# Sliding-window attention into a SwiGLU block: the first output projection by chunks of the weights, for four row groups at once

## The chip, the cores and the metric

The kernel runs on one core of a Trainium2 chip. The metric is the device time of one execution in microseconds, lower is better. A core has five engines, each with its own instruction stream: TensorE (PE, matmul; its weight loads are shown as PEld), VectorE (DVE), ScalarE (ACT), GpSimd (POOL) and SyncE (SP). They meet only through semaphores. DMA transfers are issued from the streams of POOL, SP and ACT and run beside all of them. Matmuls write to PSUM, which here is cut into eight banks of 128 x 512 float32.

## The reference

```python
# q, k, v: (8 batches, 8 heads, 576 rows, 64); float32
scores = q @ k.T / sqrt(64)                 # per batch and head
mask   = (0 <= i - j) & (i - j < 64)        # causal window of 64
attn   = softmax(where(mask, scores, -1e9)) @ v
x      = attn.transpose(0, 2, 1, 3).reshape(4608, 512)
g      = x @ w_gate                          # 512 x 1536
out    = ((g * sigmoid(g)) * (x @ w_val)) @ w_out    # w_out: 1536 x 512
```

## The kernel before, in words

The 4608 rows are worked in nine tiles of 512 (`NT = 9`). Tile t is the first 512 rows of a batch; one tile (`LAST`, t = 7) collects the last 64 rows of all eight batches. The program says "batch t" for tile t. Every instruction stream runs in the order in which the program is written (`manual_schedule`); there is no planner. Data of a tile waits only where a semaphore says so, and a buffer or PSUM bank is taken up again only when its last reader is done.

**One tile.** The eight heads go in four pairs u. `scores` (L207) multiplies the turned queries and keys of a pair into PSUM, takes the exponential on ACT into `E` and multiplies by a 0/1 mask on DVE. `totals` (L249) multiplies `E` by ones and so gets the row sums, spread over the 64 columns of a head; `log` and `invert` (L258, L261) turn them to 1/sum on ACT as exp(-ln). `mix` (L271) multiplies `E` by v, `scale` (L282) applies 1/sum on DVE and writes a quarter of `xT`; `values` is both. v is held twice: `v1` as loaded, `v2` shifted by 64 rows, since a window reaches over two blocks of 64. `gate_value` (L325) computes one of 12 columns of 128 of both gate products from `xT` in four chunks c, into a `g_ps` and a `v_ps` bank; `gate_end` (L317) makes `hT` from them with Silu (ACT) and a product (DVE). `project` (L362) multiplies `hT` by `wo` for one of four row groups s, 12 chunks of 128 into one bank `o_ps`; `project_end` (L343) copies the bank to `os_` on DVE and stores it from SP.

**PSUM.** Pool `ps_f` has two banks tagged "g" and two tagged "v" (used by g_ps, v_ps, o_ps, and by d_ps, which holds the row sums); pool `ps_a` has two tiles of two banks each, tagged "a" (scores, ao_ps, and d_ps where `wide` or `one` asks for it). Tags rotate.

**Tile 0** is the opening. The scores, totals and values are written out by hand, with `keep_warm` matmuls, whose result nobody reads, where PE would wait. From L513: the log of pair 2's sums, the shifts of v for pairs 0 to 2, values 0 and 1, the shift for pair 3, five warm-ups, chunk 0 of the first gate column, the sums of pair 3, chunk 0 of the second gate column, values 2, chunk 1 of both, values 3, chunk 2, chunk 3. Then the rest of the 12 gate columns (L533 on). Among them DVE turns the queries of batch 1 with `turn_q` (L188), after gate columns 9, 10 and 11.

**Between tile 0 and tile 1** (L557 to L574) the first projection is threaded with the attention of batch 1: scores 0 and 1; chunks 0 to 5 for row groups 0 and 1; scores 2 and 3; chunks 6 to 11 for them; the sums of pairs 0 and 1 one by one; row group 2; the sums of pairs 2 and 3 with all four mixes and scales (`finish_values`, L297); row group 3. In every later tile the loop (L576 on) does the same with whole row groups.

**Queues.** The gate weights, the keys and queries of later batches, `wo` and the v of batches 1 and 2 are issued from POOL, whose order is: gate weights, keys of batch 1, queries of batch 1 (L87), `wo` in three thirds of four chunks (L492 to L494), v of batch 1 in four parts (L495), then queries, keys and v of batch 2. POOL's transfers use eight semaphores in turn, so that each issue waits for the landing of the one eight issues earlier. SP issues the first inputs, and later the stores of the results.

Of the kernel before, what the change touches and what calls it, by code (L numbers as in the profile page):

```python
# [8 lines left out]
P = 128  # L9
FP32 = mybir.dt.float32  # L10
# [7 lines left out]
def kernel(  # L18
# [10 lines left out]
    nc = tc.nc  # L29
# [12 lines left out]
    fsb = ctx.enter_context(tc.tile_pool(name="fsb", bufs=3))  # L42
    hpool = ctx.enter_context(tc.tile_pool(name="hpool", bufs=2))
    ps_a = ctx.enter_context(tc.tile_pool(name="ps_a", bufs=2, space=PSUM))
    ps_f = ctx.enter_context(tc.tile_pool(name="ps_f", bufs=2, space=PSUM))
# [5 lines left out]
    v1 = [cst.tile([P, 4, H, D], BF16, name=f"v1{i}") for i in range(2)]  # L51
# [9 lines left out]
    def batch(t):  # L61
        return t if t < LAST else t - 1
# [7 lines left out]
    staged, queries, weights, inverse, xT, hT = {}, {}, {}, {}, {}, {}  # L70
# [55 lines left out]
    def load_v(eng, dst, t, which=range(4)):  # L126
        for i in which:
            eng.dma_start(  # L128
                dst[:, i], v[batch(t), :, P * i:P * i + P].rearrange("h r d -> r h d")
            )  # L130
# [15 lines left out]
    def cast_v(t, which=range(4), copy=nc.gpsimd.tensor_copy):  # L146
        for i in which:
            copy(v1[t % 2][:, i], staged[t, "v"][:, i])  # L148

    def shift_pair(t, u):  # L150
        hs = slice(2 * u, 2 * u + 2)
        a, b = v1[t % 2][:, :, hs], v2[t % 2][:, :, hs]
        nc.vector.tensor_copy(b[64:128, 1:4], a[64:128, 0:3])
        nc.vector.tensor_copy(b[0:64], a[0:64])

    def shift_v(t, copy, lo=0, hi=4):

        a, b = v1[t % 2], v2[t % 2]
        top = min(hi, 3)
        if top > lo:  # L160
            copy(b[64:128, lo + 1:top + 1], a[64:128, lo:top])
        copy(b[0:64, lo:hi], a[0:64, lo:hi])
# [8 lines left out]
    def weights_o(c0, c1):  # L171
        nc.gpsimd.dma_start(
            wo[:, c0:c1, :],
            moe_w_out[P * c0:P * c1].rearrange("(c r) f -> r c f", r=P),
        )
# [73 lines left out]
    def totals(t, u, d_ps):  # L249
        for h in range(2):  # L250
            nc.tensor.matmul(  # L251
                d_ps[64 * h:64 * h + 64], ones[:, 0:D], weights[t, u][:, h, :]
            )

    def room(n):
        return fsb.tile([P, 2, 512], FP32, name="r", tag="r", bufs=4)[:, 0:n]

    def log(r, d_ps):  # L258
        nc.scalar.activation(r, d_ps, AF.Ln)  # L259

    def invert(r):  # L261
        nc.scalar.activation(r, r, AF.Exp, scale=-1.0)  # L262

    def sums(t, u, d_ps):
        totals(t, u, d_ps)
        r = room(1)[:, 0]
        log(r, d_ps)
        invert(r)
        inverse[t, u] = r

    def mix(t, u, o_ps):  # L271
        E = weights.pop((t, u))
        for m in range(8):
            for h in range(2):
                nc.tensor.matmul(  # L275
                    blocks(o_ps[64 * h:64 * h + 64], t, m, m + 1),
                    (v1, v2)[m // 4][t % 2][:, m % 4, 2 * u + h, :] if t == LAST
                    else (v2, v1)[m % 2][t % 2][:, m // 2, 2 * u + h, :],
                    blocks(E[:, h, :], t, m, m + 1),
                )  # L280

    def scale(t, u, o_ps):  # L282
        if u == 0:
            xT[t] = att.tile([P, 4, 512], BF16, name="xT", tag="xT")
        nc.vector.tensor_mul(xT[t][:, u, :], o_ps, inverse.pop((t, u)))  # L285

    def values(t, u, o_ps):
        mix(t, u, o_ps)
        scale(t, u, o_ps)

    def wide(name):
        return ps_a.tile([P, 2, 512], FP32, name=name, tag="a")

    def d_tile():
        return ps_f.tile([P, 512], FP32, name="d_ps", tag="v")[:]

    def finish_values(t):  # L297
        for u in (2, 3):
            sums(t, u, d_tile())
        tiles = wide("ao_ps"), wide("ao_ps")  # L300
        for u in range(4):
            mix(t, u, tiles[u // 2][:, u % 2])
        for u in range(4):
            scale(t, u, tiles[u // 2][:, u % 2])

    def gate_part(t, ms, tiles, c):
        for m, pair in zip(ms, tiles):
            for ps, w in zip(pair, (wg, wv)):
                nc.tensor.matmul(
                    ps[:], w[:, c, P * m:P * m + P], xT[t][:, c, :],  # L310
                    start=(c == 0), stop=(c == 3),
                )

    def gate_tiles():
        return [ps_f.tile([P, 512], FP32, name=x + "_ps", tag=x) for x in "gv"]
# [19 lines left out]
    def project_part(t, ss, tiles, cs):  # L335
        for c in cs:
            for s, o_ps in zip(ss, tiles):
                nc.tensor.matmul(  # L338
                    o_ps[:], hT[t][:, c, P * s:P * s + P], wo[:, c, :],
                    start=(c == 0), stop=(c == 11),  # L340
                )

    def project_end(t, s, o_ps):  # L343
        os_ = fsb.tile([P, 512], FP32, name="os_", tag="os_", bufs=3)
        nc.vector.tensor_copy(os_[:], o_ps[:])
        rows = out[S * batch(t):S * batch(t) + 512]
        if t < TURNED:
            nc.sync.dma_start(rows.rearrange("(r e) f -> e r f", e=4)[s], os_[:])
            return
        if t == LAST:  # L350
            rows = out.rearrange("(b s) f -> b s f", s=S)[:, 512:S]
            rows = rows.rearrange("b (r e) f -> e b r f", e=16)
        else:
            rows = rows.rearrange("(r e) f -> e r f", e=16)
        for i in range(4):
            eng = nc.scalar if t == NT - 1 and i % 2 else nc.sync
            eng.dma_start(rows[4 * s + i], os_[32 * i:32 * i + 32])

    def out_tile():
        return ps_f.tile([P, 512], FP32, name="o_ps", tag="g")  # L360

    def project(t, s):  # L362
        o_ps = out_tile()
        project_part(t, (s,), (o_ps,), range(12))
        project_end(t, s, o_ps)

    def project_last(t, s):
        rows = out[S * batch(t):S * batch(t) + 512].rearrange("(r e) f -> e r f", e=16)
        os_ = fsb.tile([P, 512], FP32, name="os_", tag="os_", bufs=3)
        tiles = out_tile(), out_tile()  # L370
        for x in range(2):
            f = slice(256 * x, 256 * x + 256)
            for c in range(12):
                nc.tensor.matmul(  # L374
                    tiles[x][:, 0:256], hT[t][:, c, P * s:P * s + P], wo[:, c, f],
                    start=(c == 0), stop=(c == 11),
                )
            nc.vector.tensor_copy(os_[:, f], tiles[x][:, 0:256])
            for i in range(4):
                eng = nc.scalar if i % 2 else nc.sync  # L380
                eng.dma_start(rows[4 * s + i][:, f], os_[32 * i:32 * i + 32, f])
# [4 lines left out]
    def set_silu():  # L386
        nc.scalar.preload_act_table_set("silu_and_others")
# [18 lines left out]
    def keep_warm(n):  # L406
        for _ in range(n):
            nc.tensor.matmul(warm[0:D], ones[:, 0:D], ones[:])
# [32 lines left out]
    on_v, on_p, on_a = nc.vector.tensor_copy, nc.gpsimd.tensor_copy, nc.scalar.copy  # L441
# [49 lines left out]
    load_qk(1)  # L491
    weights_o(0, 4)  # L492
    weights_o(4, 8)
    weights_o(8, 12)  # L494
    load_v(nc.gpsimd, v1[1], 1)  # L495
    cast_v(0, (0, 1), on_v)
    scores(0, 2)
    turn_pe(3)
    d_ps, r = wide("d_ps"), room(2)
# [7 lines left out]
    def log_of(u):  # L507
        d_ps = one("d_ps")
        totals(0, u, d_ps)
        inverse[0, u] = room(1)[:, 0]  # L510
        log(inverse[0, u], d_ps)
# [2 lines left out]
    log_of(2)  # L514
    for u in range(2):
        shift_pair(0, u)
    shift_pair(0, 2)
    for u in range(2):
        values(0, u, ps_f.tile([P, 512], FP32, name="ao_ps", tag="gv"[u])[:])
    shift_pair(0, 3)  # L520
    keep_warm(5)
    pairs = [gate_tiles() for _ in range(2)]
    gate_part(0, (0,), pairs, 0)
    log_of(3)
    for u in (2, 3):
        invert(inverse[0, u])
    gate_part(0, (1,), pairs[1:], 0)
    for u in (2, 3):
        values(0, u, one("ao_ps"))
        gate_part(0, (0, 1), pairs, u - 1)  # L530
    gate_part(0, (0, 1), pairs, 3)
    set_silu()
    for m in range(12):  # L533
        if m < 2:
# [10 lines left out]
        if 5 <= m < 9:  # L545
            u = m - 5
            join(on_a, keys[:, u], raw_k[:, 2 * u:2 * u + 2])
        if 6 <= m < 10:
            u = m - 6
# [5 lines left out]
    turn_q(1, 3)  # L555

    set_exp()  # L557
    halves = out_tile(), out_tile()
    for u in range(4):
        scores(1, u)  # L560
        if u % 2:
            project_part(0, (0, 1), halves, range(3 * u - 3, 3 * u + 3))
    for s in range(2):
        project_end(0, s, halves[s])
    load_qk(2)
    load_v(nc.gpsimd, v1[0], 2)
    for i in range(4):
        shift_v(1, on_v, i, i + 1)

    for u in range(2):  # L570
        sums(1, u, d_tile())
    project(0, 2)
    finish_values(1)
    project(0, 3)  # L574

    for t in range(1, NT):  # L576
        if t > 1:
# [71 lines left out]
```

## Time and profile before

| what | value |
|---|---|
| median of 5 runs | 334.01 us (333.92 to 334.25) |
| the profiled execution's own time | 334.25 us |
| its span, first to last instruction | 332.3 us |
| granted TensorE clock, mean | 0.997 |
| PE busy | 325.9 us of the span |
| opening: start of the third gate column (m = 2) | 20.75 us |
| end of the gate columns of tile 0, start of scores 0 of batch 1 | 39.00 us |
| start of the gate columns of batch 1 | 54.15 us |
| from one tile's projection to the next, later tiles | 34.7 us (75.6, 110.3, 145.0, 179.7) |

A line of a timeline gives the start (us from the span's start), the duration, the engine, the line in the kernel, the operation with out<-in, the number of instructions merged into it, and in brackets the idle time ahead of it and what ended that. A matmul's duration reaches past the start of the next one, since they are pipelined: for a row of n matmuls the start of the next row says more than the duration. A DMA line gives the issuing queue, the number of issues, KB each, and the time from issue to landing.

### The profile page before, as it was taken

The numbers are of one execution on the slowest core, as the hardware profiler recorded it, in microseconds if no ns is written. First come the engines' busy times: TensorE is split into PE (matmuls) and PEld (weight loads), VectorE is DVE, ScalarE is ACT, GpSimd is POOL, SyncE is SP. The second block draws the span as 40 slices with busy tenths as digits, with TensorE's granted clock in tenths as the row PEclk, the third lists the DMA queues.
The fourth block names the chain that finished last, engine by engine and source line by source line (L and its number), as shares of the span: only waits on it lengthen the run. The fifth ranks groups of instructions, "written<-read, shape, count | busy, mean of one in ns | idle before, by whom it ended". The sixth has DMA issues, their size and how long they took to land.

```text
span 332.3 us, 7009 instructions
## 1 busy us (share of the span) xinstructions
PE 325.9 (98%) x2747; PEld 154.7 (47%) x2747; DVE 212.5 (64%) x326; ACT 168.2 (51%) x241; POOL 140.5 (42%) x249
## 2 busy tenths in 40 slices
PE   8999999999999999999999999999999999999995
PEld 4444435444544454445444544444444544454443
DVE  5855765586566755875678566856785576754431
ACT  5765555338533853377336743565347533953310
POOL 4954444936848984556024995264200000000000
PEclk9999999999999999999999999999999999999998
DMA  7999999999999679859922999199401320020013
GB/s 257 195 193 201 207 187 241 111 190 220 183 225 193 80 133 250 150 75 218 190 62 30 166 206 143 15 189 190 99 0 40 89 56 2 21 77 32 2 34 95
DMA packets 83249, 43.59 MB, mean 131 GB/s; under 512 B 63888, under 2 KB 77968, under 8 KB 83216
## 3 DMA queue, kind: packets, MB, share of 16 engines
q0 software_dynamic: 50416, 23.08, 56.3%
q1 hardware_dynamic: 31776, 19.02, 21.1%
q10 hardware_dynamic: 1024, 1.05, 1.1%
q8 instruction: 21, 0.34, 0.4%
q14 instruction: 12, 0.10, 0.1%
HBM read 54.00 MB, written 9.44 MB: 191 GB/s over the span
## 4 chain that ended last, share of the span: by engine, by line
PE 86%; DMA 9%; POOL 3%; issue 0%; SPq 0%; DVE 0%; POOLq 0%
PE o_ps L338 28%; PE g_ps L329 25%; PE v_ps L329 25%; DMA k_r<-in_k_dram 4%; DMA wo<-in_moe_w_out_dram 4%; PE s_ps L233 3%; PE d_ps L251 3%; PE ao_ps L275 2%; DMA q_f<-in_q_dram 1%; POOL wv L166 1%; POOL wg L166 1%; PE o_ps L374 1%; POOL v L128 1%; POOL qk_b L447 0%; POOL k_r L73 0%
## 5 line engine op out<-in xcount | busy, mean ns | idle before, releaser
L322 ACT ACTIVATE sg<-g_ps 128x512 f32<-128x512 f32 x108 | 64.4, 597 | 117.5 <-PE g_ps L329 87.5
L323 DVE TENSOR_TENSOR hT<-sg,v_ps 128x512 bf16<-128x512 f32 x108 | 74.7, 692 | 60.9 <-PE v_ps L329 59.8
L329 PE MATMUL g_ps<-xT,wg 128*128 128x512 bf16 x424 | 108.8, 379 | 0.0
L329 PE MATMUL v_ps<-xT,wv 128*128 128x512 bf16 x424 | 108.8, 379 | 0.0
L338 PE MATMUL o_ps<-wo,hT 128*128 128x512 bf16 x420 | 95.5, 380 | 0.4 <-DMA wo<-in_moe_w_out_dram 0.4
L107 POOL DMA_DIRECT2D k_s<-in_k_dram x112 | 60.6, 555 | 34.4 <-DMA q_s<-in_q_dram 22.3
L329 PEld LDWEIGHTS <-wv 128*128 128x128 bf16 x424 | 41.4, 98 | 50.1
L329 PEld LDWEIGHTS <-wg 128*128 128x128 bf16 x424 | 41.2, 98 | 49.4 <-issue 0.3
L338 PEld LDWEIGHTS <-hT 128*128 128x128 bf16 x420 | 39.0, 98 | 48.6 <-issue 4.2
L239 ACT ACTIVATE E<-s_ps 128x1024 bf16<-128x1024 f32 x36 | 35.1, 1020 | 7.8 <-PE s_ps L233 7.7
L202 DVE STREAM_TRANSPOSE kT<-k_s 128x512 bf16<-128x512 bf16 x28 | 35.9, 1281 | 0.0
L259 ACT ACTIVATE r<-d_ps 128x512 f32<-128x512 f32 (+1 forms) x35 | 21.1, 603 | 18.7 <-PE d_ps L251 18.6
L241 DVE TENSOR_TENSOR E<-E,mask 128x1024 bf16<-128x1024 bf16 x28 | 19.8, 708 | 11.8 <-ACT E L239 11.8
L87 POOL DMA_DIRECT2D q_s<-in_q_dram x28 | 15.2, 555 | 25.3 <-DVE qT L192 13.4
L285 DVE TENSOR_TENSOR xT<-ao_ps,r 128x512 bf16<-128x512 f32 x36 | 22.5, 683 | 5.2 <-PE ao_ps L275 4.0
L192 DVE STREAM_TRANSPOSE qT<-q_s 128x512 bf16<-128x512 bf16 x32 | 22.4, 703 | 0.9 <-DMA q_s<-in_q_dram 0.9
L262 ACT ACTIVATE r<-r 128x512 f32<-128x512 f32 (+1 forms) x35 | 22.4, 642 | 1.0
L148 POOL CAST v<-v_f 128x512 bf16<-128x512 f32 x20 | 12.4, 636 | 17.4 <-DMA v_f<-in_v_dram 11.9
L94 POOL DMA_DIRECT2D q_s<-in_q_dram x16 | 8.6, 628 | 9.8 <-DVE qT L192 9.8
L384 ACT ACT_TABLE_LOAD x9 | 11.5, 1283 | 2.0 <-issue 1.9
L233 PE MATMUL s_ps<-qT,kT 64*64 64x128 bf16 (+1 forms) x640 | 12.4, 211 | 0.1
L275 PEld LDWEIGHTS <-v 128*64 128x64 bf16 x576 | 10.8, 113 | 2.8 <-issue 0.8
(104 smaller groups left out, 189.6 us busy)
## 6 DMA issues: line engine op xcount, KB each, us to landing
q_s<-in_q_dram POOLq DMA_DIRECT2D x28, 248.0 KB, 7.0
k_s<-in_k_dram POOLq DMA_DIRECT2D x112, 56.0 KB, 5.1
v_f<-in_v_dram SPq DMA_DIRECT2D x22, 256.0 KB
v<-in_v_dram POOLq DMA_DIRECT2D x18, 128.0 KB, 5.3
wo<-in_moe_w_out_dram POOLq DMA_DIRECT2D x3, 512.0 KB, 12.3
v<-v SPq DMA_DIRECT2D x6, 256.0 KB
v<-v SPq DMA_DIRECT2D x6, 192.0 KB
q_f<-in_q_dram SPq DMA_DIRECT2D x4, 256.0 KB
```

The lines of the kernel that those rows point to most:

```text
L107: nc.gpsimd.dma_start(k_s[p0:p0 + 32, g, :, 0:w], k[b, a:H:2, s:s + P].rearrange("u (r e) d -> r u (e d)", e=4) [:, :, 32 * c:32 * c + w],)
L192: nc.vector.transpose(queries[t][:, u, :].rearrange("r (e x) -> r e x", e=16), staged[t][0][:, u].rearrange("r (e d) -> r e d", d=D)[:, :, ...
L202: nc.vector.transpose(dst[:, u, :].rearrange("r (g x e) -> r g e x", g=4, e=4), k_s[:, :, u].rearrange("r g (e d) -> r g e d", d=D)[:, :, ...
L233: nc.tensor.matmul(blocks(s_ps[64 * c:64 * c + 64, h], t, lo, hi), zero[r] if src is None else src[r, u, x:x + 64], blocks(qT[r], t, lo, h ...
L239: nc.scalar.activation(E[:], s_ps[:], AF.Exp, scale=0.125)
L259: nc.scalar.activation(r, d_ps, AF.Ln)
L262: nc.scalar.activation(r, r, AF.Exp, scale=-1.0)
L285: nc.vector.tensor_mul(xT[t][:, u, :], o_ps, inverse.pop((t, u)))
L322: nc.scalar.activation(sg[:], g_ps[:], AF.Silu)
L323: nc.vector.tensor_mul(hT[t][:, m, :], sg[:], v_ps[:])
L329: nc.tensor.matmul(ps[:], w[:, c, P * m:P * m + P], xT[t][:, c, :], start=(c == 0), stop=(c == 3),)
L338: nc.tensor.matmul(o_ps[:], hT[t][:, c, P * s:P * s + P], wo[:, c, :], start=(c == 0), stop=(c == 11),)
```

## The change

The POOL queue issues v of batch 1 ahead of the last third of `wo`. In the opening, pair 2's shift moves behind values 0 and 1, the sums of pair 3 and both inversions come before the gate parts, one warm-up is left of five, chunks 0 and 1 of both first gate columns run in a row, then values 2 and 3, then chunks 2 and 3. The first projection takes four banks ("g", "v", "g", "v") and runs chunk by chunk for all four row groups: chunks 0 to 3 between scores 1 and 2, chunks 4 to 6 after scores 3, then the sums of batch 1 as two pairs (one logarithm and one inversion for each), chunks 7 to 9, the four mixes and scales, chunks 10 and 11. The four banks are then copied out together, two on ACT and two on DVE. The shifts of v go by pairs instead of by row blocks. `os_` has four buffers instead of three.

```diff
     def finish_values(t):
         for u in (2, 3):
             sums(t, u, d_tile())
+        mix_all(t)
+
+    def mix_all(t):
         tiles = wide("ao_ps"), wide("ao_ps")
         for u in range(4):
             mix(t, u, tiles[u // 2][:, u % 2])
...
-    def project_end(t, s, o_ps):
-        os_ = fsb.tile([P, 512], FP32, name="os_", tag="os_", bufs=3)
-        nc.vector.tensor_copy(os_[:], o_ps[:])
+    def project_end(t, s, o_ps, copy=nc.vector.tensor_copy):
+        os_ = fsb.tile([P, 512], FP32, name="os_", tag="os_", bufs=4)
+        copy(os_[:], o_ps[:])
...
     weights_o(0, 4)
     weights_o(4, 8)
+    load_v(nc.gpsimd, v1[1], 1)
     weights_o(8, 12)
-    load_v(nc.gpsimd, v1[1], 1)
...
     for u in range(2):
         shift_pair(0, u)
-    shift_pair(0, 2)
     for u in range(2):
         values(0, u, ps_f.tile([P, 512], FP32, name="ao_ps", tag="gv"[u])[:])
-    shift_pair(0, 3)
-    keep_warm(5)
-    pairs = [gate_tiles() for _ in range(2)]
-    gate_part(0, (0,), pairs, 0)
+    for u in (2, 3):
+        shift_pair(0, u)
     log_of(3)
     for u in (2, 3):
         invert(inverse[0, u])
-    gate_part(0, (1,), pairs[1:], 0)
+    keep_warm(1)
+    pairs = [gate_tiles() for _ in range(2)]
+    for c in range(2):
+        gate_part(0, (0, 1), pairs, c)
     for u in (2, 3):
         values(0, u, one("ao_ps"))
-        gate_part(0, (0, 1), pairs, u - 1)
-    gate_part(0, (0, 1), pairs, 3)
+    for c in range(2, 4):
+        gate_part(0, (0, 1), pairs, c)
...
     set_exp()
-    halves = out_tile(), out_tile()
+    tiles = [ps_f.tile([P, 512], FP32, name="o_ps", tag=x) for x in "gvgv"]
+
+    def columns(c0, c1):
+        project_part(0, range(4), tiles, range(c0, c1))
+
     for u in range(4):
         scores(1, u)
-        if u % 2:
-            project_part(0, (0, 1), halves, range(3 * u - 3, 3 * u + 3))
-    for s in range(2):
-        project_end(0, s, halves[s])
+        if u == 1:
+            columns(0, 4)
+    columns(4, 7)
+    for u in (0, 2):
+        d_ps, r = wide("d_ps"), room(2)
+        for i in range(2):
+            totals(1, u + i, d_ps[:, i])
+            inverse[1, u + i] = r[:, i]
+        log(r, d_ps[:])
+        invert(r)
     load_qk(2)
     load_v(nc.gpsimd, v1[0], 2)
-    for i in range(4):
-        shift_v(1, on_v, i, i + 1)
-
-    for u in range(2):
-        sums(1, u, d_tile())
-    project(0, 2)
-    finish_values(1)
-    project(0, 3)
+    for u in range(4):
+        shift_pair(1, u)
+    columns(7, 10)
+    mix_all(1)
+    columns(10, 12)
+    for s in range(4):
+        project_end(0, s, tiles[s], on_a if s < 2 else on_v)
```

More of the change, by code (lines that the diff above doesn't have):

```diff
@@ L368, in project_last @@
         rows = out[S * batch(t):S * batch(t) + 512].rearrange("(r e) f -> e r f", e=16)
-        os_ = fsb.tile([P, 512], FP32, name="os_", tag="os_", bufs=3)
+        os_ = fsb.tile([P, 512], FP32, name="os_", tag="os_", bufs=4)
         tiles = out_tile(), out_tile()
```

## The prediction

> **What bounds the kernel now.** First the busy shares and the chain of waits on the page: is it one engine all the way?
>
> ```profile
> PE 325.9 (98%) x2747; PEld 154.7 (47%) x2747; DVE 212.5 (64%) x326; ACT 168.2 (51%) x241; POOL 140.5 (42%) x249
> PE 86%; DMA 9%; POOL 3%; issue 0%; SPq 0%; DVE 0%; POOLq 0%
> ```
>
> TensorE (PE) is busy 98% of the span, and the chain is PE for 86%; the 9% of DMA lie ahead of 42.3 us, at loads of the opening. So only two things can pay: less PE work, or PE waits removed. The change removes next to no work (four warm-up matmuls), so I look for waits, in PE's timeline of the first projection (start, duration, what, idle before it and its releaser):
>
> ```profile
> 39.64 0.22 PE L233 MATMUL s_ps<-qT,zero 64*64 64x64 bf16 x2 [0.22 <-DVE qT L192]
> 39.65 0.41 PE L233 MATMUL s_ps<-qT,kT 64*64 64x128 bf16 x16
> 39.99 1.90 PE L338 MATMUL o_ps<-wo,hT 128*128 128x512 bf16 x8
> 42.28 1.02 PE L338 MATMUL o_ps<-wo,hT 128*128 128x512 bf16 x4 [0.38 <-DMA wo<-in_moe_w_out_dram]
> ...
> 43.82 2.92 PE L338 MATMUL o_ps<-wo,hT 128*128 128x512 bf16 x12
> 46.67 0.62 PE L251 MATMUL d_ps<-E,ones 128*64 128x512 bf16 x4
> 47.30 2.75 PE L338 MATMUL o_ps<-wo,hT 128*128 128x512 bf16 x12
> 49.98 0.62 PE L251 MATMUL d_ps<-E,ones 128*64 128x512 bf16 x4
> 50.44 1.18 PE L275 MATMUL ao_ps<-E,v 128*64 128x64 bf16 x64
> 51.55 2.76 PE L338 MATMUL o_ps<-wo,hT 128*128 128x512 bf16 x12
> 54.15 1.03 PE L329 MATMUL g_ps<-xT,wg 128*128 128x512 bf16 x4
> ```
>
> A full matmul repeats every 0.216 us (51.55 to 54.15 over 12 is 0.217). Eight from 39.99 end their pace at 41.72, the next starts at 42.28: 0.56 us of wait for the second third of wo. The twelve at 43.82 should give way at 46.41 plus the usual 0.09 of a change of tile shape (49.89 to 49.98 is a clean one); they do so at 46.67: another 0.17, where column 8, the first of the last third, is reached. So 39.99 to 54.15 (14.16) holds 0.73 of waits for wo and 13.43 of work. The DMA view of the windows in which they are issued gives the landing times:
>
> ```profile
> wo<-in_moe_w_out_dram POOLq DMA_DIRECT2D x1, 512.0 KB, 13.6
> v<-in_v_dram POOLq DMA_DIRECT2D x1, 128.0 KB, 11.9
> ```
>
> The last wo, issued at 31.21, lands at 44.8; the last v, issued at 36.31, at 48.2. In the same way wo's first two land at 39.7 and 42.2: about 2.6 us for each third, in the order of issue, and 3.4 for the four v.
>
> **The change, part by part.** (1) *The opening.* Today five warm-ups cover the wait for the first xT; then gate_part, totals and values alternate:
>
> ```profile
> 14.18 1.25 PE L408 MATMUL warm<-ones 128*64 128x512 bf16 x5
> 15.36 0.39 PE L309 MATMUL g_ps<-xT,wg 128*128 128x512 bf16 x1
> ...
> 19.69 0.38 PE L309 MATMUL g_ps<-xT,wg 128*128 128x512 bf16 x1
> ```
>
> Changed: pair 2's shift (0.7 us on DVE) no longer stands ahead of the first scale, which starts when 1/sum is there, about 14.2 instead of 14.52. PE goes straight to the totals of pair 3, which wait for its exponential (ACT, 14.04 + 1.00): 15.10. One warm-up and a change of tile later chunk 0 starts at 15.64; eight matmuls to 17.37; values 2 from about 17.46, values 3 from 17.71. Chunk 2 then waits for its scale: values 2 end at 17.90, the 0.69 us scale ends near 18.7, chunk 2 starts at 18.75 and chunk 3 at 19.6, against 19.69 today. So the opening is worth -0.1, and I bound it by +-0.3: two PE gaps (about 14.3 to 15.1 and 18.1 to 18.75) are now covered by nothing, where today two gate parts stand between the values.
>
> None of it reaches the end. The queries of the next batch are turned on DVE as their DMA lands:
>
> ```profile
> 37.69 0.71 DVE L192 STREAM_TRANSPOSE qT<-q_s 128x512 bf16<-128x512 bf16 x1 [0.90 <-DMA q_s<-in_q_dram]
> 38.32 0.65 DVE L323 TENSOR_TENSOR hT<-sg,v_ps 128x512 bf16<-128x512 f32 x1
> 38.89 0.69 DVE L192 STREAM_TRANSPOSE qT<-q_s 128x512 bf16<-128x512 bf16 x1
> ```
>
> That transfer's place in the POOL queue is untouched, so scores(1,1) starts at 39.64 in both kernels. It swallows all that the opening gains, and up to about 0.25 of what it may lose (the idle before 39.64). Without that cover each 0.1 counts in full.
>
> Here a rule speaks against the change: the Trainium skill, "TensorE: Matmul & The Clock Gate", "Why this matters for your kernels", says that idle gaps over about 3 us drop TensorE to half its clock. The opening shows that pace: six 512-column matmuls in 2.77 us from 1.77, where five take 1.25 later. By the rule, gaps of 0.8 and 0.65 us are too short to trip it: 0. If they did, a window of 3.4 us (the page's figure) holds 16 matmuls at 0.216, which would take twice as long: +3.4. I take 0; no gap after the warm-up in this trace is as long, so it cannot prove it.
>
> (2) *v ahead of the last third of wo.* Four POOL issues (0.88 us each) move ahead of one of 0.74. Each POOL issue waits for the landing eight issues earlier, so the slots keep their times: v at 31.2 to 35.0, the last wo at 36.3. The bytes ahead are the same; v should land at 43 to 45.6 and the last wo at 48.2, where the last v stands today. Behind them q and k of batch 2 keep their place; nothing on PE waits for those before 60 us. SP's stores move from 47-55 to 53-56, in the same order.
>
> (3) *The projection, four row groups by chunk.* Same matmuls (48 o_ps, 8 totals, 64 mix), same number of shape changes: work 13.4. From 39.99:
> - columns 0-3: 16 x 0.216, to 43.44; needs only the first third (39.7). Its fourth tile waits for hT's last product (about 40.2) and is used at 40.64: free.
> - scores 2 and 3: 0.68, to 44.12. Columns 4-6: 12, to 46.71; the second third is there since 42.2, so the 0.56 is gone.
> - eight totals: 0.09 + 4 x 0.216 + 0.20 for the change back = 1.15, to 47.86.
> - column 7, to 48.72. Column 8 needs the last third (48.2): free by 0.5, so the 0.17 is gone. Columns 8-9, to 50.45.
> - mix: 0.09 + 1.11, from 50.54 to 51.65. It needs the shifts (DVE, four pairs at about 0.75 from 46.7: 49.75) and, for pairs 2 and 3 at 51.04, the second paired logarithm. ACT: logs of 1.02 and inverses of 1.06 alternate from 47.45, so it ends at 50.5. Free by 0.5.
> - columns 10-11: 8, to 53.39.
>
> All eight PSUM banks are in use then, so the gate of batch 1 waits for the first o_ps to be copied out. Its last matmul starts at 52.53 and ends at 52.91 (they last 0.38); the copy is new on ACT, nearest row 0.60 (Ln and Silu of a 128x512 f32 PSUM tile): to 53.55, PE at 53.60. Price 0.21; bounds 0 (a copy that keeps up) and 0.5 (one of DVE's 0.69, begun late). The other three copies (ACT 54.1, DVE 54.5 and 55.2 after its four scales) are done before their banks are due (54.5, 55.3, 56.2). Silu's table load ends at 55.4 behind the copies; its first bank is due at 57.0. All hidden.
>
> (4) *A fourth os_ buffer* is worth 0: at the end the copies start as o_ps ends.
>
> **Sum**, against the profiled execution (334.25: span 332.3 and 1.95 around it): -0.56 - 0.17 + 0.21 = about -0.5; the gate starts at 53.6 instead of 54.15, and all behind it is PE-bound, so it moves along: 333.7. The median is 0.24 below that execution. If the 0.24 is around the work, the median comes to 333.46; if the usual run just waits less for wo, the gain is smaller. I take 333.5, -0.15%.
>
> **Rivals.**
> - *The waits go and the bank is free in time* (or q lands earlier than in this execution): -0.75 to -1.1, 333.0. For it: ACT is idle from 51.6, a copy could be quicker than Ln; against: it is in series behind the last matmul.
> - *The last wo is late*, the one on the other side of the line. v's packets are small, and q's and k's issues now run earlier behind them; if the last third lands after 48.72 each 0.1 costs 0.1. Break-even with today is 49.25; over 0.2% slower from 49.9. At 50.5 it costs 1.8 - 0.5: 335.3. Against it: the row of landings in order of issue, and the same bytes ahead.
> - *The opening loses its cover*: a clock drop costs 3.4 less the 0.25 of cover and the 0.5: 336.6. Against it the rule and the gap lengths above.
> - *Nothing shows*: the 0.73 is mostly bad luck of this execution, 333.9.
>
> **How the numbers follow.** 0.2% (0.67 us) is about what a measurement of this kernel can tell from no change: faster is below 333.34, slower above 334.68. My forecast 0.62 (332.9 to 333.9; two thirds of it within 0.2%, a third below); bank free 0.13, faster; late wo 0.10, two thirds of it slower; lost cover 0.08, slower; nothing shows 0.07, same. Faster 0.33, same 0.52, slower 0.15. The range 332.9 to 334.7 leaves out the far ends of the slow cases and of the fast one.
>
> **What would show it.** No idle for wo on PE between 40 and 54; the last wo landing before 48.7; the first gate matmul near 53.6, released by an ACT copy; scores(1,1) still at about 39.6; chunk 2 of the opening behind xT with PE idle 0.5; 34.7 us from batch to batch afterwards, as now. I am wrong if the gate starts at or after 54.15, if matmuls repeat at 0.43 after 14 us, or if a later batch takes longer.

## The result

| | before | changed |
|---|---|---|
| median, us | 334.02 (51 runs) | 333.19 (30 runs) |
| ratio of the times, 95% interval | | 0.9975 (0.9967 to 0.9983) |
| profiled execution, us | 334.25 | 333.23 |
| its span, us | 332.3 | 331.4 |
| third gate column of tile 0 starts | 20.75 | 20.75 |
| first o_ps matmul of the projection | 39.99 | 39.62 |
| gate of batch 1 starts | 54.15 | 53.21 |

The change is worth -0.83 us, or -0.25% (interval -0.33% to -0.17%). It is faster; whether by more than the 0.2% line, the interval leaves open.

The page of the changed kernel first: its busy shares and its chain of waits.

```profile
PE 324.4 (98%) x2743; PEld 154.9 (47%) x2743; DVE 211.4 (64%) x325; ACT 168.6 (51%) x239; POOL 140.0 (42%) x249
PE 96%; ACT 1%; DMA 1%; DVE 1%; issue 0%
```

The bound is the same engine, but the chain has changed hands: DMA had 9% of it, all ahead of 42.3 us, and now has 1%. The chain ran through the loads of `wo`, and no longer does. PE's timeline of the first projection in the changed kernel shows why:

```profile
39.01 0.41 PE L233 MATMUL s_ps<-qT,kT 64*64 64x128 bf16 x16
39.27 0.22 PE L233 MATMUL s_ps<-qT,zero 64*64 64x64 bf16 x2
39.27 0.41 PE L233 MATMUL s_ps<-qT,kT 64*64 64x128 bf16 x16
39.62 3.63 PE L341 MATMUL o_ps<-wo,hT 128*128 128x512 bf16 x16
...
43.77 2.77 PE L341 MATMUL o_ps<-wo,hT 128*128 128x512 bf16 x12
46.47 1.05 PE L251 MATMUL d_ps<-E,ones 128*64 128x512 bf16 x8
47.45 2.76 PE L341 MATMUL o_ps<-wo,hT 128*128 128x512 bf16 x12
50.15 1.20 PE L275 MATMUL ao_ps<-E,v 128*64 128x64 bf16 x64
51.28 1.90 PE L341 MATMUL o_ps<-wo,hT 128*128 128x512 bf16 x8
53.21 1.02 PE L332 MATMUL g_ps<-xT,wg 128*128 128x512 bf16 x4
```

No line between 39 and 54 has an idle time for `wo`. From the first o_ps matmul to the gate are 13.59 us. The last eight matmuls keep their pace to 53.01 (51.28 + 8 x 0.216), yet the gate starts at 53.21: 0.20 us, the wait for the first bank. Its copy is in ACT's timeline:

```profile
52.57 0.58 ACT L348 COPY os__907<-o_ps 128x512 f32<-128x512 f32 x1 [1.33 <-PE o_ps L341]
53.05 0.59 ACT L348 COPY os__910<-o_ps 128x512 f32<-128x512 f32 x1
53.66 1.28 ACT L390 ACT_TABLE_LOAD   x1
```

The copy ends at 53.15, the gate follows 0.06 later. And in DVE's timeline the queries come earlier than in the first profile, where the turn started at 37.69:

```profile
37.31 0.71 DVE L192 STREAM_TRANSPOSE qT<-q_s 128x512 bf16<-128x512 bf16 x1 [0.52 <-DMA q_s<-in_q_dram]
```

That is why scores 1 follows scores 0 at once at 39.27. The last third of `wo`, issued at 36.27, lands 11.8 later, at 48.1:

```profile
wo<-in_moe_w_out_dram POOLq DMA_DIRECT2D x1, 512.0 KB, 11.8
```

Column 8 needs it at 48.3 (47.45 + 4 x 0.216): in time, but by only 0.2.

### The profile page after: what moved, and what is told of

It is laid out like the page before. It is cut to its first block, busy times and chain, and to the rows that moved or that the text cites. A ratio compares the mean times of both kernels' runs of the same rounds, so it can differ in the third digit from the quotient of the medians.

```text
span 331.4 us, 6997 instructions
## 1 busy us (share of the span) xinstructions
PE 324.4 (98%) x2743; PEld 154.9 (47%) x2743; DVE 211.4 (64%) x325; ACT 168.6 (51%) x239; POOL 140.0 (42%) x249
## 4 chain that ended last, share of the span: by engine, by line
PE 96%; ACT 1%; DMA 1%; DVE 1%; issue 0%
PE o_ps L341 28%; PE g_ps L332 28%; PE v_ps L332 28%; PE s_ps L233 3%; PE d_ps L251 3%; PE ao_ps L275 3%; PE tp L180 1%; DMA q_f<-in_q_dram 1%; PE o_ps L377 1%; PE g_ps L312 1%; PE v_ps L312 1%; PE warm L411 0%; ACT r L262 0%; ACT r L259 0%; ACT E L239 0%; PE s_ps L225 0%
## 5 line engine op out<-in xcount | busy, mean ns | idle before, releaser
L241 DVE TENSOR_TENSOR E<-E,mask 128x1024 bf16<-128x1024 bf16 x28 | 19.6, 699 | 11.8 <-ACT E L239 11.7
L148 POOL CAST v<-v_f 128x512 bf16<-128x512 f32 x20 | 12.4, 635 | 19.3 <-DMA v_f<-in_v_dram 11.8
L251 PE MATMUL d_ps<-E,ones 128*64 128x512 bf16 x72 | 11.5, 391 | 0.7 <-ACT E L239 0.7
## 6 DMA issues: line engine op xcount, KB each, us to landing
wo<-in_moe_w_out_dram POOLq DMA_DIRECT2D x3, 512.0 KB, 11.8
```

The source lines that it names most:

```text
L251: nc.tensor.matmul(d_ps[64 * h:64 * h + 64], ones[:, 0:D], weights[t, u][:, h, :])
```

## The experiments

Three theories stood against each other. The forecast's: scores 1 waits for the queries in both kernels, so both projections start at the same time and the opening counts in neither. The new one, A: the old projection runs at the pace at which the thirds of `wo` land, and whatever comes ahead of that, the wait for the queries too, lies in the shadow of the landings; the changed one has no such shadow, and starts when PE or the queries are ready, whichever is later. And B: the new opening makes the queries land earlier, and that is the gain beyond the forecast. Each kernel is compared with the kernel before, run on the same chip.

**The opening alone, and the projection alone.** The first is the kernel before with the hunk of the opening (from `shift_pair(0, 2)` to the last `gate_part`); the second is the changed kernel with that hunk undone.

```diff
 # opening_only, against before; projection_only has the opposite, against the changed kernel
...
-    keep_warm(5)
...
+    keep_warm(1)
...
+    for c in range(2):
+        gate_part(0, (0, 1), pairs, c)
     for u in (2, 3):
         values(0, u, one("ao_ps"))
-        gate_part(0, (0, 1), pairs, u - 1)
-    gate_part(0, (0, 1), pairs, 3)
+    for c in range(2, 4):
+        gate_part(0, (0, 1), pairs, c)
```

> The kernel before with the new opening alone (one warm-up, chunks 0 and 1 in a row, then the values); projection and POOL queue as before. Theory A (the landings of wo set the pace of the old projection, and everything ahead of them lies in their shadow): no change, 334.0 +-0.1, whatever the opening ends at; the third gate column starts at 20.75 +-0.1. Theory B (the new opening makes the queries of batch 1 land earlier): also about 334.0, but the turn of the first queries starts near 37.3 in the trace instead of 37.7. Lost cover or a clock drop in the opening: the third gate column after 21.2.

Measured: 333.97, ratio 0.9998 (0.9988 to 1.0008); the third gate column at 20.79. No change, as all three had it. Its turn of the queries started at 36.84, but that is not the opening's doing, as the next run shows.

> The changed kernel with the old opening (five warm-ups, gate parts between the values). Theory A: all of the gain is here, -0.7 to -0.9 against before, 333.2. Theory B: without the new opening the queries land late, near 37.7, and scores 1 waits for them: -0.5, 333.5.

Measured: 333.31, ratio 0.9985 (0.9969 to 1.0002), -0.7 in the medians; queries turned at 37.38, first o_ps at 39.69, gate at 53.28, or 13.59 for the projection again. The times alone don't separate the theories (the interval is wide, and it reaches no change). Against B stands the trace: with the old opening the queries were as early as in the changed kernel. One trace is little where they scatter so much, but all of them together say the same: the turn starts at 36.79 to 37.69 in the five traces with the old opening (37.25 in the mean), and at 36.72 to 37.62 in eight with the new one (37.17). So the gain is in the projection, as far as medians of 333.31 and 333.19 can tell.

**More work ahead of the projection.** Eight 128-column matmuls more among gate columns 6 and 7, which PE was expected to need 0.43 us for (in the traces scores 0 starts 18.70 after the third gate column instead of 18.25).

```diff
             transposes(tp, keys[:, u])
+            if m < 8:
+                transposes(tp, keys[:, u])
```

> The kernel before with the four transposes of k for pairs 0 and 1 of batch 1 done twice (eight more 128-column matmuls among gate columns 6 and 7; the same result), which puts 0.43 us more of work on PE ahead of the first projection. Theory A: swallowed by the waits for wo (0.73 in the trace): 334.0 to 334.1. My forecast's step (a wait for the queries of about 0.25 is all the cover): +0.2. No cover: +0.43.

Measured: 333.84, ratio 0.9995 (0.9986 to 1.0004). Nothing of the 0.43 shows (the interval ends at +0.13 us). This is the run that decides: PE comes to the old projection later, and waits for `wo` by so much less. PE's timeline of it:

```profile
40.12 2.76 PE L338 MATMUL o_ps<-wo,hT 128*128 128x512 bf16 x11
...
43.40 2.81 PE L338 MATMUL o_ps<-wo,hT 128*128 128x512 bf16 x11
```

Twelve matmuls in a row where the kernel before had eight, a wait and four (one of the twelve is missing from the records). This trace shows more than its share, though: in this execution the whole queue ran ahead, the last third of `wo` was issued at 30.74 instead of 31.21 and landed at 44.2 instead of 44.8, and the gate starts at 53.62. What holds in all four traces of the old projection with the old queue order is that the gate follows that landing by 9.3 to 9.4: landings at 44.8, 44.9, 44.6 and 44.2, gates at 54.15, 54.22, 53.93 and 53.62 (the kernel before twice, opening_only, before_late). And the waits for `wo`, 0.7 to 1.0 in the three without the extra work, are long enough to take in 0.43.

> The same eight matmuls in the changed kernel. Theory A: no wait for wo is left to swallow them, and the queries are on time to within 0.1 in its trace: +0.35 to +0.43, 333.6. My forecast's step (scores 1 waits for the queries in both kernels): +0.1 to +0.2.

Measured: 333.43, ratio 0.9986 (0.9977 to 0.9995); against the changed kernel's 333.19 about +0.24. So the same 0.43 seems to cost the changed kernel about half its size, and the old one nothing. The size is loose: against the second set of the changed kernel (333.26, below) it is +0.17, and the intervals overlap. A number between A's and the forecast's is what the traces lead one to expect. Counted from the start of the turn, the queries let the projection start 2.31 us later; counted from the start of scores 0, PE does 0.59 later; and it cannot start before the first third of `wo` is there. Put 0.43 more on PE in each of the seven traces of the changed projection that have neither the extra work nor the last run's moves, and the start moves by 0 to 0.43, by 0.24 in the mean (an estimate from these traces): in some executions the queries are late enough to cover the extra work, in others they aren't.

**How late are the queries?** The two kernels once more, for a second trace of each.

> The kernel before, for a second trace. If the queries' late landing in the first profile (turn at 37.7) was particular to that execution, the turn starts between 36.7 and 37.4 as in the other traces, scores 1 follows scores 0 without a wait, the wait for wo's second third is by so much longer, and the gate of batch 1 starts at 53.8 to 54.1. If it belongs to the kernel before: 37.6 to 37.8 again. Time 334.0.

> The changed kernel once more, beside the two below on the same chip: 333.2; turn of the queries between 36.7 and 37.4, gate of batch 1 at 52.9 to 53.3.

Measured: 334.03 and 333.26 (ratios 1.0002 and 0.9982, 0.9973 to 0.9992). The repeats settle it, and not quite as expected. PE's timeline of the kernel before, second trace:

```profile
39.79 1.90 PE L338 MATMUL o_ps<-wo,hT 128*128 128x512 bf16 x8
42.04 1.02 PE L338 MATMUL o_ps<-wo,hT 128*128 128x512 bf16 x4 [0.35 <-DMA wo<-in_moe_w_out_dram]
...
44.92 1.89 PE L338 MATMUL o_ps<-wo,hT 128*128 128x512 bf16 x8 [0.30 <-DMA wo<-in_moe_w_out_dram]
```

And of the changed kernel, second trace:

```profile
39.51 0.22 PE L233 MATMUL s_ps<-qT,zero 64*64 64x64 bf16 x2 [0.31 <-DVE qT L192]
...
53.45 1.02 PE L332 MATMUL g_ps<-xT,wg 128*128 128x512 bf16 x4
```

This time the queries were early in the kernel before (turn at 37.16) and late in the changed one (37.55, outside the expected window), so the lateness belongs to the execution and not to the kernel. In the kernel before, the early start bought nothing: the projection began 0.20 earlier than in the first trace, column 8 began at 44.92, and the gate at 54.2, where it had been. In the changed kernel, the late queries cost what they were late: start 39.86, gate 53.45. From start to gate the changed kernel took 13.59 in all five traces that have its projection as it stands: 39.62, 39.69, 39.35 and 39.86 to 53.21, 53.28, 52.94 and 53.45 (the changed kernel, projection_only, v_behind further down, and this one), and 39.81 to 53.40 in after_late. From column 8 to the gate the old one takes 9.30 in the three that show a wait for it (54.15, 54.22 and 53.93 less 44.85, 44.92 and 44.63).

**The place of v.**

```diff
 # v_behind, against the changed kernel; v_alone has the opposite, against before
-    load_v(nc.gpsimd, v1[1], 1)
     weights_o(8, 12)
+    load_v(nc.gpsimd, v1[1], 1)
```

> The changed kernel with v of batch 1 issued behind the last third of wo again, as before. Theory A: the last third lands at 44.8, long before its use at 48.3; v lands at 48.2 and its shifts end about 50.7, just ahead of each pair's mix: no difference to the changed kernel, 333.2 +-0.15. Rival (v ahead is what makes the mix free): the mix at 50.15 waits for the shifts and the time goes up by 0.3 to 1.

Measured: 333.08, ratio 0.9977 (0.9967 to 0.9987), the same as the changed kernel. DVE waits for v (0.84 and 0.49), its shifts end at 49.8, and the mix starts at 49.87 without a wait. That part of the change is worth nothing either way; the new projection uses the last third of `wo` so late that either order does.

> The kernel before with v of batch 1 moved ahead of the last third of wo, nothing else. The old projection reaches chunk 8 at 44.7, the last third now lands at 48.1: PE idles 3.4 where it idled 0.2: +3.2, 337.2. Rival (landings do not follow the order of issue): under +1.

Measured: 340.05, ratio 1.0180 (1.0166 to 1.0194): +6.0, nearly twice what was expected. The wait was sized well; what it set off was left out. PE's timeline, and then PE's windows (length, PE busy, granted clock as a share of full, DMA share, GB/s), of this kernel:

```profile
43.35 1.04 PE L338 MATMUL o_ps<-wo,hT 128*128 128x512 bf16 x4
47.83 0.59 PE L338 MATMUL o_ps<-wo,hT 128*128 128x512 bf16 x1 [3.44 <-DMA wo<-in_moe_w_out_dram]
...
59.61 1.03 PE L329 MATMUL g_ps<-xT,wg 128*128 128x512 bf16 x4
```

```profile
45.50:46.00 0.50, 0.00 (x0) 1.00 1.21 202
46.00:46.50 0.50, 0.00 (x0) 0.89 1.24 218
46.50:47.00 0.50, 0.00 (x0) 0.50 1.16 212
...
51.00:53.00 2.00, 2.00 (x7) 0.50 1.38 199
53.00:53.50 0.50, 0.50 (x3) 0.78 1.20 288
53.50:54.00 0.50, 0.50 (x4) 1.00 1.08 221
```

In the idle time the clock falls to half: within the slice from 46.0 to 46.5, where a mean of 0.89 puts the step at 46.4, and it stays at 0.50 for more than 5 us after the matmuls are back, to about 53.2. From column 8 to the gate it took 11.78 (47.83 to 59.61) instead of 9.30: +2.5. With column 8 later by 3.0 (47.83 against 44.85) that makes the 5.5 by which the gate is late.

**The bank wait.** All four copies on DVE; and chunks 10 and 11 row group by row group, twice.

```diff
 # all_dve
-        project_end(0, s, tiles[s], on_a if s < 2 else on_v)
+        project_end(0, s, tiles[s], on_v)
 # rows_last, rows_again
-    columns(10, 12)
+    for s in range(4):
+        project_part(0, (s,), (tiles[s],), range(10, 12))
```

> The changed kernel with all four banks copied out on DVE. DVE is at the four scales until 53.4, so the first copy ends near 54.0 and the gate starts there instead of 53.2: +0.8, 334.0, all of the gain gone. Rival (the bank wait is not set by the copy's engine): +0.1 at most.

Measured: 334.28, ratio 1.0006 (0.9994 to 1.0019): +1.1 against the changed kernel, all of the gain gone. PE's timeline of it has the wait, with the copy as its releaser:

```profile
54.21 1.02 PE L332 MATMUL g_ps<-xT,wg 128*128 128x512 bf16 x4 [0.91 <-DVE os__907 L348]
```

DVE's timeline has the reason: its four scales stand ahead of the copy.

```profile
51.07 2.48 DVE L285 TENSOR_TENSOR xT<-ao_ps,r 128x512 bf16<-128x512 f32 x4 [2.14 <-PE ao_ps L275]
53.47 0.68 DVE L348 COPY os__907<-o_ps 128x512 f32<-128x512 f32 x1
```

Start to gate is 14.47 instead of 13.59, or +0.88; the rest of the 1.1 is within the scatter. So the two copies on ACT are as much a part of the gain as the order of the chunks.

> The changed kernel with chunks 10 and 11 of the projection run row group by row group, so that the first bank is complete after 2 of the 8 matmuls and not after 5. If the wait of the gate for the copy of the first bank is worth the 0.2 that the trace shows, it goes: -0.2 against the changed kernel, 333.0, and the gate starts right behind the last o_ps. If something else holds the gate (the scales of xT, the second bank): no change, 333.2.

> Chunks 10 and 11 row group by row group, beside the changed kernel: 0.2 less than the changed kernel of this call, if the bank wait is what goes; 0.0 if the difference in the first comparison was chance.

Measured: 333.00 and 332.99, ratios 0.9979 (0.9968 to 0.9990) and 0.9976 (0.9966 to 0.9986); -0.2 and -0.3 against the changed kernel's 333.19 and 333.26, alike in both sets though neither is clear of noise alone. The traces give the step without the scatter: start to gate 13.39 and 13.40 (39.23 to 52.62, 40.02 to 53.42) instead of 13.59. The wait for the copy is what goes, as the gate now follows the last eight matmuls at their pace (51.68 + 8 x 0.216 = 53.41, in rows_again):

```profile
51.68 1.90 PE L341 MATMUL o_ps<-wo,hT 128*128 128x512 bf16 x8
53.42 1.03 PE L332 MATMUL g_ps<-xT,wg 128*128 128x512 bf16 x4
```

**With the shadow gone, the opening counts.** On top of the row groups:

```diff
-    for c in range(2):
-        gate_part(0, (0, 1), pairs, c)
+    gate_part(0, (0, 1), pairs, 0)
     for u in (2, 3):
         values(0, u, one("ao_ps"))
-    for c in range(2, 4):
+    for c in range(1, 4):
         gate_part(0, (0, 1), pairs, c)
...
-        if m >= 9:
-            turn_q(1, m - 9)
+        for u in {9: (0, 1), 11: (2,)}.get(m, ()):
+            turn_q(1, u)
```

> Chunks 10 and 11 row group by row group, and two more moves: in the opening values 2 and 3 run between chunk 0 and chunk 1, so that chunk 1 covers the scale that chunk 2 waits for (the third gate column then starts at 20.2 to 20.3 instead of 20.75); and the turn of the second pair's queries goes ahead of the tenth hT product. With no wait for wo left, the opening's gain should now reach the projection, until the first third of wo (39.2 to 39.7) stops it: -0.1 to -0.4 against the row-by-row kernel alone. If the landings of the queries or of wo already set the pace: 0.0, with a new PE wait for them near 39.

Measured: 332.69, ratio 0.9967 (0.9955 to 0.9979) in five executions. That is 0.30 below the row-by-row kernel on the same chip, but the two intervals overlap, so this step alone is not clear of noise. PE's timeline has the end of the opening and the start of the projection:

```profile
15.07 0.39 PE L312 MATMUL g_ps<-xT,wg 128*128 128x512 bf16 x1
...
19.53 1.02 PE L332 MATMUL g_ps<-xT,wg 128*128 128x512 bf16 x4
...
38.47 0.37 PE L233 MATMUL s_ps<-qT,kT 64*64 64x128 bf16 x14
39.27 1.04 PE L341 MATMUL o_ps<-wo,hT 128*128 128x512 bf16 x4 [0.43 <-DMA wo<-in_moe_w_out_dram]
```

The third gate column, at 19.53, is 1.22 earlier than in the first trace of the changed kernel, and half of that is luck of the execution: chunk 0, ahead of which nothing was moved, starts at 15.07 where the changed kernel's first trace has 15.70. The move itself is the distance from chunk 0 to the third column: 4.46, against 5.04 to 5.06 in all eight other traces with the new opening, or -0.6. Only 0.35 of the 1.22 reaches the projection (39.27 against 39.62). PE loses 0.40 more than elsewhere between the third gate column and scores 0, and then it waits 0.43 for the first third of `wo`, which now sets the start. Against before the medians differ by -1.3. How much of the 0.3 each of the two moves brings was not taken apart.

## Why the prediction was right, and where its size was off

- **The waits for wo go (-0.56 and -0.17).** Right: between the first o_ps and the gate none is left in any trace of the changed projection. The size was a single execution's: start to gate less the 13.43 of work gives 0.73, 1.00 and 0.87 in three traces of the old projection, and 0.07 in before_late.
- **The projection's own work and the bank wait (13.40 + 0.21 from the first o_ps to the gate).** Right to 0.02: 13.59 in five traces; 0.20 of it is the wait for the copy, 0.19 came back in both row-by-row traces, and the copy took 0.58 where 0.60 was put. The forecast's bounds of 0 and 0.5 for it held with ACT; on DVE it is 0.9 more, since DVE's scales come first.
- **The projection starts at 39.64 + 0.35 = 39.99 in both kernels.** This is the step that was mis-sized. The start was read off one trace in which the queries were late. For the kernel before it doesn't matter, because its gate follows the landing of the last third of `wo` wherever the projection starts (0.43 us more work ahead of it cost nothing). For the changed kernel the start is the whole matter: 39.35 to 39.86 in four traces without extra work, 39.63 in the mean, 0.36 earlier than 39.99. It is set by the last of three arrivals, PE, the queries and the first third of `wo`, which lie within a few tenths of each other. A wait that is in the shadow of another was carried over to a kernel in which the other is gone, as if it were of a fixed size.
- **So the opening reaches the end in neither kernel.** Wrong for the changed one, by the same step: of 0.43 us more ahead of the projection about 0.2 came through. That a shorter opening with an earlier turn brings 0.3 is what the medians say, but not clear of noise.
- **The opening itself, -0.1 +- 0.3.** In the two first traces it was 0.0, the third gate column at 20.75 in both. Over all traces it was about -0.2, within the bounds: 20.75 to 20.95 with the old opening (five, 20.82 in the mean), 20.16 to 20.87 with the new (eight, 20.60); tight, with its own opening, is left out. Chunk 2 waits 0.60 for its scale and starts at 18.82, against 18.75 worked out.
- **v ahead of the last third of wo, free.** Right, by a smaller margin than thought (0.2 instead of 0.5 in the first trace, 0.1 to 1.0 in the others with this order), and not needed.
- **All behind the gate moves along; the fourth os_ buffer is worth nothing.** The later projections are 34.7 us apart as before; nothing showed of the buffer, which was not tried alone.
- **The sum.** -0.5 was forecast and -0.83 measured. The gates in the traces account for it: 53.22 in the mean of the four traces of the changed projection, against 54.15, 54.22 and 53.93 (the opening alone) of the old one, 54.10 in the mean: 0.88. With before_late's 53.62 among the old ones it is 0.76, so this account is good to about 0.1. The rival that bundled a free bank with earlier queries (333.0) was half of what took place: the bank was not free, the queries were earlier. The 333.19 lies nearer to it than to the 333.5, and on the side of the 0.2% line that the forecast gave 0.33 and not 0.52.
- **The rivals on the other side.** The late landing of the last third of `wo` didn't come (48.1), but v_alone shows what it would have cost, with the clock. The lost cover of the opening didn't come: the changed opening has PE gaps of 0.65 and 0.60, and the matmuls behind them keep to 0.216. The rule weighed there (the Trainium skill, "TensorE: Matmul & The Clock Gate", "Why this matters for your kernels": gaps over about 3 us) fits the gap of 3.44, in which the clock fell to 0.50. But it fell 2.0 us into the gap, so in this run a gap well under 3 us would have met it. The price put on such a drop, +3.4, was worked out wrongly: the 3.4 us that it took, at half the clock, hold 8 matmuls of 0.43 and not 16, and so cost 1.7. Measured were 2.5, because the slow stretch with PE at work lasted 5.4 us.

## What to carry to other kernels

When a change removes a wait, look at what stood in that wait's shadow: waits ahead of it that cost nothing before are on the path now, and work that was pointless to shorten is worth its time, up to the next arrival that sets the start. Do not take such a hidden wait's size from a single execution when a DMA sets it; a second trace of the unchanged kernel would have shown 0.5 us of play. When four accumulations are finished together, the last pass should run bank by bank, and the first copies should go to an engine that is free at that moment.

## What the runs showed of the hardware

- A PE gap can cost more than itself: in v_alone, after the last matmul ended at 44.4, the granted clock fell to half at about 46.4, 2.0 us later, and came back at about 53.2, 5.4 us after the matmuls resumed. The gap of 3.4 us cost 2.5 more. In the other traces no gap behind the first matmuls is longer than 0.91 us, and the granted clock reads 1.00 up to 330 us. Nothing between 0.91 and 3.44 was tried.
- In the opening six 512-column matmuls from 1.77 take 2.77 us, twice the later pace, while the granted clock of that stretch is shown as 1.00. So the row of granted clocks shows a drop later on, but not this slow start; there the spacing of the matmuls has to be read. The slow start doesn't always end at the same place: eight transposes at about 4.8 us take 0.89 to 1.04 in eleven traces, and 0.62 in rows_last, rows_again and tight. In two of these three PE also reaches chunk 0 earlier (15.11 and 15.07, against 15.45 to 15.73 in the other traces with the new opening); in rows_again a wait of 0.70 for queries of the first batch comes between.
- The landing of the last part of the queries, some 10 us after its issue, with the row of DMA shares at 9 throughout that stretch, differed by 1 us between executions of kernels with the same queue order up to that point (landings from 36.6 to 37.6, turns from 36.72 to 37.69). The first third of `wo`, next in that queue, scattered as much: 39.1 to 40.0.
